# Where a weight matrix is split, and on which engine sums are formed, in a fused attention and two-layer kernel

## Chip, cores, metric

The kernel runs on one core of one Trainium2 chip. The metric is the device time of one execution in microseconds (us). Five engines work side by side: PE (TensorE, matrix products; the profile shows its weight loads as PEld), DVE (VectorE), ACT (ScalarE), POOL (GpSimd) and SP (SyncE, which here issues the DMAs).

## What is computed

Attention is followed by two feed-forward layers on the same 2304 tokens of width 512:

```python
x = attention(q, k, v, s)          # 4 x 8 heads, 576 rows, head width 64
h = x @ w_in                       # layer 1: 512 -> 2048
g = s * max(h, 0)**2 + b
x = g @ w_out                      # 2048 -> 512
a, b = x @ w_a, x @ w_b            # layer 2: 512 -> 1536, twice
out = (a * b) @ moe2_w_out         # 1536 -> 512
```

All is in float32. A product in full float32 is made of three products in the engine's reduced format: each operand is split into a high part (a cast on ACT) and a low part (operand minus high part, on DVE), and hi*hi, hi*lo and lo*hi are added up in PSUM. In layer 2 the products are moreover done by a scheme with seven block products in place of eight, as Strassen's, so sums and differences of blocks of the operands are needed as well, and these are split too.

## The kernel before

**Planner.** The kernel hands a list of operations, each with an engine, an estimated cost and a priority (a position in time, smaller first), to `Plan`. `Plan.order` (L120) plays them through once, with these costs, and takes at each moment the ready operation of the smallest priority; the instructions go out in that order. So the order on each engine is fixed before the kernel runs: an instruction whose operand is late holds up all that stands behind it on its engine. Buffers belong to a `Tag` (L31), which is a number of slots; a tag that is `in_order` gives its slots out in the order in which the buffers were declared, and an operation that needs a slot is not ready until one is free.

**Stages.** Up to 511 us attention and the first chunks of layer 1 share the engines. From 511 to 619 us layer 1 does its last two chunks (`last_two`, L898): 16 slices, in each 12 matmuls of `hh` and 12 of `yy`, of 512 columns. Between a slice's `hh` and its `yy` stand a relu on ACT (L830), a product on DVE (L841), an addition with cast on ACT (L844) and a subtraction on DVE (L846). This stage is called the tail of layer 1 below. From 619 to 886 us a and b are computed, in six rounds `i` of about 44 us: in each, `group(i, m, j)` (L1103) and `conv` (L1162) multiply the tokens by one slice of w_a (m = 0) and of w_b (m = 1). From 886 to 1016 us follows the product with moe2_w_out for two halves `j` of the tokens (`g_pair`, L1296), seven block products of 3 x 12 matmuls each, and from 1016 us on the rest of the tokens (`g_conv`).

**Slices of weights.** `w2_slice` (L1002) brings one slice of 1 MB in: a DMA into `t_wraw` (2 slots), a decoding from float64 in two or three passes (`decode`, L434: ACT L450, DVE or ACT L457/L453, DVE L459 and L462), four sums of blocks on POOL (L1017) into `sm` (`t_sum`, 1 slot), and then for `wa` (the blocks) and `ws` (the sums) a cast on ACT and a subtraction on DVE (L1021, L1022). Both land in `t_ring`, 4 slots. It is called for 12 slices of w_a and w_b, where round `i` prepares round `i + 1`, and by `wo_slice` (L1190) for the six slices of moe2_w_out; there 8 DMAs of 256 KB (L1197) then write `wa` and `ws` to `wo_dr` in DRAM, from where `wo_load` (L1229) takes them for the last product. In the kernel before, all six `wo_slice` have positions 432 to 462 and so lie in the tail of layer 1 with the two slices of round 0.

**Slots of `t_w`.** This tag has 16 slots of 8 KB per partition, in order. In layer 1 they hold its weights; in the rounds they hold 7 + 7 split blocks of tokens (`X`) and one more for `conv`, so 15; in the last product they hold `wo` (12) and the split blocks of a*b (`G`).

**Sums of a*b.** `g_sums` (L1269) takes four blocks R of a*b for each half `j` and each of three `ip`, and forms five sums on POOL (L1278 through `sub`, and L1290), each of 128 x 1024 elements: R00 = R01 - R00, d2 = R11 - R00, R01 = R11 - R01, R10 = R10 - R11, R10 = R10 + R00. Seven operands per `ip` go through `g_split` (L1262): a cast on ACT, a subtraction on DVE (L1265). The partial results of the seven products are added on DVE out of PSUM (L1331).

Of the kernel before, what the change touches and what calls it, by code (L numbers as in the profile page):

```python
# [14 lines left out]
ALU = mybir.AluOpType  # L15
# [12 lines left out]
PE, DVE, ACT, POOL, SP = "PE", "DVE", "ACT", "POOL", "SP"  # L28
# [205 lines left out]
def fused_kernel(  # L234
# [15 lines left out]
    nc = tc.nc  # L250
# [5 lines left out]
    NF1 = w1.shape[0]  # L256
# [7 lines left out]
    op = plan.op  # L264

    def as32(ap):
        return ap.bitcast(F32)
# [21 lines left out]
    def tag(pool, shape, dt, bufs, name, in_order=True):  # L289
        def make(n):  # L290
            p = pools[pool] if isinstance(pool, str) else pool
            return p.tile(shape, dt, tag=name, bufs=bufs, name=n)

        return Tag(make, bufs, in_order)
# [9 lines left out]
    t_w = tag(wpool, [P, 2, 2, DM], F32R, NF1, "w")  # L304
# [517 lines left out]
    for p in range(NPAIR):  # L822
        x_t[NCK - 1, p] = Buf(t_x, f"xlast{p}")
        op(SP, 0.4, 431.0, lambda p=p: nc.sync.dma_start(as32(x_t[NCK - 1, p].t), as32(xl_dr.t[p])),
           r=[xl_dr], w=[x_t[NCK - 1, p]], dma=262144)
# [147 lines left out]
    NFH = NF2 // 2  # L973
    t_ring = tag("ph2", [P, 4, 2, 2 * P], F32R, 4, "ring")
    t_wraw = tag("ph2", [P, 2, DM, 2], U32, 2, "wraw")
    t_sum = tag("ph2", [P, 4, 2 * P], F32, 1, "wsum")
    t_yraw = tag("ph2", [P, 2, 512], F32, 2, "yraw")
    t_su = Tag(lambda n: moe.tile([P, 2, 512], F32, tag="g", bufs=3, name=n), 3, False, t_g)
# [15 lines left out]
    def after(n0, deps):  # L994
        for o in plan.ops[n0:]:
            for d in deps:
                d.next.append(o)
                o.wait += 1

    ring = {}  # L1000

    def w2_slice(m, i, pos, n, src):  # L1002

        raw, sm = Buf(t_wraw, f"raw2_{m}{i}"), Buf(t_sum, f"sm{m}{i}")
        wa, ws = Buf(t_ring, f"wa{m}{i}"), Buf(t_ring, f"ws{m}{i}")
        ring[m, i] = wa, ws
        n0 = len(plan.ops)
        words = decode(raw, src, n % 2 == 1, pos, pos)

        def blk(q):  # L1010
            return words(1).bitcast(F32).rearrange("p a (b n) -> p (a b) n", n=2 * P)[:, q]

        for z, (q, x, y, f_) in enumerate((
            (0, lambda: blk(3), lambda: blk(2), ALU.add), (1, lambda: sm.t[:, 0], lambda: blk(0), ALU.subtract),
            (2, lambda: blk(0), lambda: blk(3), ALU.subtract), (3, lambda: blk(1), lambda: sm.t[:, 1], ALU.subtract),
        )):
            op(POOL, 0.75, pos + 0.1, lambda q=q, x=x, y=y, f_=f_: nc.gpsimd.tensor_tensor(out=sm.t[:, q], in0=x(), in1=y(), op=f_),  # L1017
               r=[(raw, "hi"), *([(sm, 0)] if q == 1 else [(sm, 1)] if q == 3 else [])], w=[(sm, q)])
        for t, k_, rd, src in ((wa, 0.0, (raw, "hi"), lambda: words(1).bitcast(F32).rearrange("p a (b n) -> p (a b) n", n=2 * P)),
                               (ws, 0.2, sm, lambda: sm.t)):  # L1020
            op(ACT, 1.08, pos + k_, lambda t=t, src=src: nc.scalar.copy(t.t[:, :, 0], src()), r=[rd], w=[(t, 0)])  # L1021
            op(DVE, 1.12, pos + k_, lambda t=t, src=src: nc.vector.tensor_tensor(  # L1022
                out=t.t[:, :, 1], in0=src(), in1=as32(t.t[:, :, 0]), op=ALU.subtract
            ), r=[rd, (t, 0)], w=[(t, 1)])
        after(n0, ready2)
# [162 lines left out]
    wo_dr = dram_buf([4, NFH // 2, P, 2, 2, 2, 2 * P], F32R, "wo_dr")  # L1188

    def wo_slice(i, pos):  # L1190
        w2_slice("o", i, pos, i, w2o[i])
        n0 = len(plan.ops)
        for g, names in enumerate(GROUPS):
            for z, n_ in enumerate(names):
                t, q = PLACE[n_]
                t = ring["o", i][t]
                op(SP, 0.35, pos + 0.5, lambda g=g, z=z, t=t, q=q: nc.sync.dma_start(  # L1197
                    as32(wo_dr.t[g, i // 2, :, z, i % 2]), as32(t.t[:, q])
                ), r=[t], w=[(wo_dr, (g, i, z))], dma=262144)
        after(n0, ready2)  # L1200

    PER = 60.0
    for i in range(NFH):
        wo_slice(i, 432.0 + 6.0 * i)
    for m in range(2):
        w2_slice(m, 0, 440.0 + 10.0 * m, m, w2ab[0, m])
    x_pair(0, 500.0)
    x_pair(1, BASE + 1.0)
    x_conv(BASE + 2.0)
    for i in range(NFH):  # L1210
        p0 = BASE + PER * i
        for m in range(2):
            group(i, m, 0, p0 + 8.0 * m)
        c0, g0 = (16.0, 24.0) if i + 1 < NFH else (32.0, 16.0)
        for m in range(2):
            conv(i, m, p0 + c0 + 4.0 * m)
        for m in range(2):
            group(i, m, 1, p0 + g0 + 8.0 * m)
        if i + 1 < NFH:
            for m in range(2):  # L1220
                w2_slice(m, i + 1, p0 + 4.0 + 20.0 * m, m, w2ab[i + 1, m])

    EP = BASE + PER * NFH
    ORDER = (("11", "11", 0), ("d2", "s2", 1), ("21", "12", 0), ("d3", "s3", 1), ("d1", "s1", 2), ("d4", "22", 1), ("22", "s4", 2))
# [37 lines left out]
    def g_split(j, n_, ip, pos, rd, src):  # L1262
        hl = G[j, n_, ip]
        op(ACT, 1.0, pos, lambda: nc.scalar.copy(hl.t[:, :, 0], src()), r=[rd], w=[(hl, 0)], late=0.1)
        op(DVE, 1.12, pos, lambda: nc.vector.tensor_tensor(  # L1265
            out=hl.t[:, :, 1], in0=src(), in1=as32(hl.t[:, :, 0]), op=ALU.subtract
        ), r=[rd, (hl, 0)], w=[(hl, 1)], late=0.08)

    def g_sums(j, pos):  # L1269
        for ip in range(NIP):  # L1270
            pr = pos + 0.2 * ip
            r = {(fh, T): R[j, fh, T, ip] for fh in range(2) for T in range(2)}
            key = {k_: (v_[0], v_[1][1]) for k_, v_ in r.items()}
            ap = {k_: v_[2] for k_, v_ in r.items()}
            d2 = Buf(t_sum if ip == 0 else t_yraw, f"d2{j}{ip}")

            def sub(k_, o, a, b, okey, rds):
                op(POOL, 2.3, pr + k_, lambda: nc.gpsimd.tensor_tensor(out=o(), in0=a(), in1=b(), op=ALU.subtract),  # L1278
                   r=rds, w=[okey])

            d2v = lambda d2=d2: d2.t.rearrange("p a n -> p (a n)").rearrange("p (a n) -> p a n", a=2)
            g_split(j, "11", ip, pr, key[0, 0], ap[0, 0])
            sub(0.0, ap[0, 0], ap[0, 1], ap[0, 0], key[0, 0], [key[0, 1]])
            sub(0.1, d2v, ap[1, 1], ap[0, 0], d2, [key[1, 1], key[0, 0]])
            g_split(j, "d2", ip, pr + 6.0, d2, d2v)
            g_split(j, "21", ip, pr + 12.0, key[1, 0], ap[1, 0])
            sub(10.0, ap[0, 1], ap[1, 1], ap[0, 1], key[0, 1], [key[1, 1]])
            g_split(j, "d3", ip, pr + 18.0, key[0, 1], ap[0, 1])
            sub(20.0, ap[1, 0], ap[1, 0], ap[1, 1], key[1, 0], [key[1, 1]])
            op(POOL, 2.3, pr + 20.1, lambda a=ap: nc.gpsimd.tensor_tensor(out=a[1, 0](), in0=a[1, 0](), in1=a[0, 0](), op=ALU.add),  # L1290
               r=[key[0, 0]], w=[key[1, 0]])
            g_split(j, "d1", ip, pr + 24.0, key[0, 0], ap[0, 0])
            g_split(j, "d4", ip, pr + 30.0, key[1, 0], ap[1, 0])
            g_split(j, "22", ip, pr + 36.0, key[1, 1], ap[1, 1])
# [233 lines left out]
```

## Time and profile before

| | us |
|---|---|
| median of 3 runs | 1036.35 |
| lowest and highest run | 1035.92, 1040.34 |
| the profiled execution, its own time | 1038.79 |
| span of its trace, first to last instruction | 1037.10 |
| PE busy | 982.1 |
| DVE busy | 776.2 |
| ACT busy | 552.1 |
| POOL busy | 219.2 |

The profile gives one execution, with each instruction's start, length, and what ended the idle time before it. PE's busy time is modelled from pipelined matmuls, so that one at full pace still shows small overlaps; the distance between the starts of blocks of matmuls is the better measure of pace. The granted clock of PE is 1.00 where it is at full speed.

### The profile page before, as it was taken

How to read it: one execution, taken by the hardware profiler on the slowest of the kernel's cores; microseconds unless marked ns; L12 is line 12 of the kernel's file. 1: busy time of each engine (PE TensorE's matmuls, PEld its weight loads, DVE VectorE, ACT ScalarE, POOL GpSimd, SP SyncE). 2: the span in 40 equal slices, each digit the busy share in tenths (PEclk: the TensorE clock that was granted, in tenths of full speed). 3: DMA queues.
4: the chain of work that ended last, by engine and by line, in shares of the span. 5: the costliest groups of instructions: out<-in, count | busy, mean ns of one | idle time of the engine just before them, and what ended most of it. 6: DMA issues, size and time to landing. Idle time of an engine off the chain costs nothing. (4 is left out here: it accounts for less than half of the span.)

```text
span 1037.1 us, 17316 instructions
## 1 busy us (share of the span) xinstructions
PE 982.1 (95%) x6664; PEld 877.6 (85%) x6664; DVE 776.2 (75%) x1153; ACT 552.1 (53%) x1025; POOL 219.2 (21%) x173
## 2 busy tenths in 40 slices
PE   4699999999999999999999879999999999999798
PEld 4598999999999999999877657888888888778678
DVE  6889764578788888887489977757576567877872
ACT  4779974568787878786356543313133121423331
POOL 4121001100000000000244524112011113955920
PEclk9999999999999999999999999999999999999899
DMA  9958523557769687866588633413222356955013
GB/s 231 225 159 226 143 82 67 120 134 172 153 137 188 135 159 157 159 142 116 188 307 295 206 101 109 170 68 122 88 86 95 128 172 244 365 188 177 0 61 102
DMA packets 159249, 160.12 MB, mean 154 GB/s; under 512 B 115008, under 2 KB 126016, under 8 KB 153280
## 3 DMA queue, kind: packets, MB, share of 16 engines
q1 hardware_dynamic: 159168, 159.03, 54.7%
q8 instruction: 52, 0.85, 0.3%
q14 instruction: 29, 0.24, 0.1%
HBM read 95.20 MB, written 37.52 MB: 128 GB/s over the span
## 5 line engine op out<-in xcount | busy, mean ns | idle before, releaser
L861 PE MATMUL h<-x_all,w 128*128 128x256 f32 x1344 | 180.3, 286 | 1.8 <-ACT r L830 1.0
L881 PE MATMUL y<-g,w 128*128 128x256 f32 x1344 | 181.1, 287 | 0.0
L861 PEld LDWEIGHTS h<-x_all,w 128*128 128x128 f32 x1344 | 168.8, 193 | 3.1 <-ACT r L830 1.2
L881 PEld LDWEIGHTS y<-g,w 128*128 128x128 f32 x1344 | 167.1, 191 | 1.5
L576 PE MATMUL av<-tr,vt 128*64 128x320 f16 (+4 forms) x1120 | 65.0, 274 | 12.7 <-DMA tr<-hl 7.5
L576 PEld LDWEIGHTS <-vt 128*64 128x64 bf16 x1120 | 54.5, 116 | 23.8 <-issue 8.5
L1095 PE MATMUL b<-x,wa 128*128 128x512 f32 x288 | 72.8, 390 | 0.0
L540 ACT ACTIVATE hl<-p,rc 128x256 f16<-128x256 f32 (+3 forms) x128 | 66.0, 559 | 4.4 <-DVE rc L557 4.4
L542 DVE SCALAR_TENSOR_TENSOR hl<-p,rc,hl 128x256 f16<-128x256 f32 (+3 forms) x128 | 65.8, 548 | 0.1
L1017 POOL TENSOR_TENSOR sm<-raw 128x256 f32<-128x256 f32 x24 | 26.4, 1100 | 183.9 <-DVE ws L1022 157.8
L1095 PEld LDWEIGHTS b<-x,wa 128*128 128x128 f32 x288 | 53.7, 188 | 10.8
L926 PE MATMUL yy<-gg,w 128*128 128x512 f32 x192 | 50.5, 408 | 11.2 <-DVE gg L846 8.6
L1130 ACT COPY su<-b 128x512 f32<-128x512 f32 x24 | 14.1, 587 | 85.2 <-PE b L1095 85.2
L1318 PE MATMUL pb<-g,wo 128*128 128x512 f32 x216 | 53.8, 403 | 5.4 <-DVE g L1265 2.8
L1120 DVE TENSOR_TENSOR su<-b,su 128x512 f32<-128x512 f32 x48 | 32.8, 687 | 31.6 <-PE b L1095 31.6
L926 PEld LDWEIGHTS yy<-gg,w 128*128 128x128 f32 x192 | 36.5, 194 | 23.2 <-DVE gg L846 11.9
L1318 PEld LDWEIGHTS pb<-g,wo 128*128 128x128 f32 x216 | 41.9, 195 | 14.9 <-ACT psu L1335 3.1
L1095 PE MATMUL b<-x0d,ws 128*128 128x512 f32 x216 | 54.2, 390 | 0.3 <-DVE su L1120 0.3
L1095 PE MATMUL b<-x1d,ws 128*128 128x512 f32 x216 | 53.7, 390 | 0.4 <-DVE su L1120 0.4
L626 PE MATMUL s<-kq 66*128 66x256 f32 (+1 forms) x128 | 43.5, 465 | 10.0 <-POOL vt L361 7.6
L914 PE MATMUL hh<-x_all,w 128*128 128x512 f32 x192 | 47.6, 400 | 3.1 <-ACT rr L830 3.1
L783 DVE TENSOR_REDUCE nm<-s 128x1 f32<-128x512 f32 (+1 forms) x64 | 36.9, 619 | 15.5 <-PE s L779 15.5
(379 smaller groups left out, 2087.6 us busy)
## 6 DMA issues: line engine op xcount, KB each, us to landing
raw<-in_w_dram SPq DMA_DIRECT2D x16, 1024.0 KB
raw<-in_w2ab_dram SPq DMA_DIRECT2D x12, 1024.0 KB
ab_dr<-at_all SPq DMA_DIRECT2D x24, 512.0 KB
wo<-wo_dr SPq DMA_DIRECT2D x12, 1024.0 KB
R<-ab_dr SPq DMA_DIRECT2D x24, 512.0 KB
rk<-in_k_dram SPq DMA_DIRECT2D x16, 576.0 KB
raw_o<-in_w2o_dram SPq DMA_DIRECT2D x6, 1024.0 KB
wo_dr<-wao SPq DMA_DIRECT2D x24, 256.0 KB
```

The lines of the kernel that those rows point to most:

```text
L540: nc.scalar.activation(o, i_, AF.Copy, scale=r_)
L542: nc.vector.scalar_tensor_tensor(out=o, in0=i_, scalar=r_, in1=place()[:, k0:k1, 0, :cols], op0=ALU.mult, op1=ALU.subtract)
L576: nc.tensor.matmul(ap.t[64 * h : 64 * h + 64, :w], vap(j, h, vi), t[:, j, a, h, :w], start=j == 0 and m == 0, stop=j == nkt - 1 and m == 4,)
L626: nc.tensor.matmul(o, qt[:66, x, h, ti * P : (ti + 1) * P], kt[:66, x, h, :w], start=True, stop=False)
L783: op(DVE, DVE_PS(w), pr, lambda c=c, w=w, nmx=nmx, bank=banks[c]: nc.vector.tensor_reduce(out=nmx.t[:, c : c + 1], in_=bank.t[:, :w], axis ...
L861: nc.tensor.matmul(o, w[:, wi, c, :], x_t[ck, c].t[:, xi], start=m == 0, stop=m == 3 * KC - 1)
L881: nc.tensor.matmul(o, w1_t[2 * fp + j].t[:, 1, wi, e * P : (e + 1) * P], g.t[:, gi, j], start=fp == 0 and e % 2 == 0 and j == wi == gi == ...
L914: nc.tensor.matmul(hp.t, w[:, wi, c, :], x_all[:, :, c, xi, :], start=m == 0, stop=m == 3 * KC - 1)
L926: nc.tensor.matmul(y_ps[e].t, w1_t[f].t[:, 1, wi, e * P : (e + 1) * P], g.t[:, gi].rearrange("p a n -> p (a n)"), start=f == m == 0, stop= ...
L1095: nc.tensor.matmul(o, wt.t[:, q, wi, kt * P : (kt + 1) * P], hl_of(kt, xi), start=first and n == 0, stop=last and n == 5, skip_group_check ...
L1120: op(DVE, 0.64, e, lambda: nc.vector.tensor_tensor(out=dst(), in0=bank.t, in1=a(), op=ALU.add), r=[bank, *reads], w=[key], late=0.08)
L1318: nc.tensor.matmul(banks[bi][dp].t, wv(i2, wi, dp), hl.t[:, i2, xi, :], start=n_ in fresh and ip == i2 == m == 0, stop=ip == NIP - 1 and i ...
```

## The change

- `wo_slice` is called from within the rounds: slice 0 in round 0, 1 in round 1, 2 and 3 in round 2, 4 in round 3, 5 in round 4, none in round 5, at positions 14 (and 36) after the start of the round, in place of 432 to 462.
- Its `wa` and `ws` come from a new tag `t_wv`, a view of `t_w` that shares its slots and its queue, in place of `t_ring`. As `t_w` has 15 of 16 slots taken in the rounds, `ws` of a slice can be written when the four DMAs of its `wa` have ended.
- `w2_slice` forms its sums on the engine that it is told: VectorE for the two slices of round 0, POOL for all others, with estimated costs of 0.42 and 0.95 in place of 0.75.
- `g_sums` forms its sums on VectorE, with an estimated cost of 1.12 in place of 2.3, and four of them in place of five: R10 = R10 - d2 in place of (R10 - R11) + R00. d2 is so read later, and its buffer held longer.

```diff
--- before
+++ after
@@ -973,6 +973,8 @@
     t_wraw = tag("ph2", [P, 2, DM, 2], U32, 2, "wraw")
+    t_wv = Tag(lambda n: t_w.make(n).rearrange("p a b n -> p (a b n)").rearrange("p (q z n) -> p q z n", q=4, z=2), NF1, True, t_w)
+    t_wv.queue = t_w.queue
@@ -999,10 +1001,10 @@
-    def w2_slice(m, i, pos, n, src):
+    def w2_slice(m, i, pos, n, src, home, sums_on):
 
         raw, sm = Buf(t_wraw, f"raw2_{m}{i}"), Buf(t_sum, f"sm{m}{i}")
-        wa, ws = Buf(t_ring, f"wa{m}{i}"), Buf(t_ring, f"ws{m}{i}")
+        wa, ws = Buf(home, f"wa{m}{i}"), Buf(home, f"ws{m}{i}")
@@ -1014,7 +1016,8 @@
-            op(POOL, 0.75, pos + 0.1, lambda q=q, x=x, y=y, f_=f_: nc.gpsimd.tensor_tensor(out=sm.t[:, q], in0=x(), in1=y(), op=f_),
+            f_eng, cost = (nc.gpsimd, 0.95) if sums_on == POOL else (nc.vector, 0.42)
+            op(sums_on, cost, pos + 0.1, lambda q=q, x=x, y=y, f_=f_, f_eng=f_eng: f_eng.tensor_tensor(out=sm.t[:, q], in0=x(), in1=y(), op=f_),
@@ -1188,7 +1191,7 @@
     def wo_slice(i, pos):
-        w2_slice("o", i, pos, i, w2o[i])
+        w2_slice("o", i, pos, i, w2o[i], t_wv, POOL)
@@ -1200,10 +1203,9 @@
     PER = 60.0
-    for i in range(NFH):
-        wo_slice(i, 432.0 + 6.0 * i)
+    WO_AT = ((0,), (1,), (2, 3), (4,), (5,), ())
     for m in range(2):
-        w2_slice(m, 0, 440.0 + 10.0 * m, m, w2ab[0, m])
+        w2_slice(m, 0, 440.0 + 10.0 * m, m, w2ab[0, m], t_ring, DVE)
@@ -1218,7 +1220,9 @@
             for m in range(2):
-                w2_slice(m, i + 1, p0 + 4.0 + 20.0 * m, m, w2ab[i + 1, m])
+                w2_slice(m, i + 1, p0 + 4.0 + 20.0 * m, m, w2ab[i + 1, m], t_ring, POOL)
+        for n, io in enumerate(WO_AT[i]):
+            wo_slice(io, p0 + 14.0 + 22.0 * n)
@@ -1275,7 +1279,7 @@
             def sub(k_, o, a, b, okey, rds):
-                op(POOL, 2.3, pr + k_, lambda: nc.gpsimd.tensor_tensor(out=o(), in0=a(), in1=b(), op=ALU.subtract),
+                op(DVE, 1.12, pr + k_, lambda: nc.vector.tensor_tensor(out=o(), in0=a(), in1=b(), op=ALU.subtract),
@@ -1286,9 +1290,7 @@
-            sub(20.0, ap[1, 0], ap[1, 0], ap[1, 1], key[1, 0], [key[1, 1]])
-            op(POOL, 2.3, pr + 20.1, lambda a=ap: nc.gpsimd.tensor_tensor(out=a[1, 0](), in0=a[1, 0](), in1=a[0, 0](), op=ALU.add),
-               r=[key[0, 0]], w=[key[1, 0]])
+            sub(20.0, ap[1, 0], ap[1, 0], d2v, key[1, 0], [d2])
```

## Rows read from the trace of the kernel before

**Rows 1.** Busy time of each engine in the three stages; columns in the first line

```profile
core 0: us, PE busy (x) PEld busy (x) DVE busy (x) ACT busy (x) POOL busy (x), PEclk, DMA share, GB/s
511.05:619.39 108.34, 93.96 (x387) 73.65 (x385) 98.72 (x96) 59.06 (x79) 50.41 (x36) 0.97 0.63 217
619.39:886.12 266.73, 264.57 (x1297) 223.63 (x1296) 183.01 (x230) 72.27 (x93) 54.56 (x49) 1.00 0.37 134
886.12:1015.99 129.87, 119.73 (x507) 97.13 (x506) 100.97 (x62) 45.34 (x48) 79.05 (x26) 0.96 0.42 154
```

**Rows 2.** PE's waits, 495 to 620 us: us in total, times, longest

```profile
PE yy L926 <- DVE gg L846: 8.6, 7, 2.1
PE hh L914 <- ACT rr L830: 3.1, 1, 3.1
PE yy L926 <- ACT gg L844: 2.6, 2, 2.1
```

**Rows 3.** Timeline of PE, near both ends of the tail: start, length, [idle before <- releaser]

```profile
519.81 7.34 PE L914 MATMUL hh<-x_all,w 128*128 128x512 f32 x24 [3.13 <-ACT rr L830]
...
615.18 4.37 PE L926 MATMUL yy<-gg,w 128*128 128x512 f32 x11 [0.28 <-DVE gg L846]
```

**Rows 4.** Chain of work that ended last, its longest piece: start, length, what

```profile
822.40 47.64 PE b L1095 x210
```

**Rows 5.** Timeline of POOL, then of ACT, ahead of PE's first wait in the tail

```profile
515.44 1.72 POOL L1017 TENSOR_TENSOR smo<-raw_o,smo 128x256 f32<-128x256 f32 x1
...
517.19 1.04 ACT L1021 CAST wso<-smo 128x1024 fp32r<-128x1024 f32 x1 [3.97 <-POOL smo L1017]
```

**Rows 6.** Instructions on raw_o alone, 495 to 620: DVE, ACT, POOL busy

```profile
495.00:620.00 125.00, 28.51 (x21) 17.00 (x15) 32.90 (x24) 0.97 0.63 218
```

**Rows 7.** The same for wso: DVE and ACT busy

```profile
495.00:620.00 125.00, 7.31 (x6) 6.33 (x6) 0.97 0.63 218
```

**Rows 8.** Busy time in a stretch of layer 1; columns as in Rows 1

```profile
300.00:480.00 180.00, 180.00 (x1700) 172.97 (x1698) 150.20 (x310) 142.93 (x298) 2.04 (x10) 1.00 0.75 151
```

**Rows 9.** Busy time in one round; columns as in Rows 1

```profile
734.60:778.50 43.90, 43.90 (x218) 37.30 (x217) 29.47 (x39) 11.83 (x14) 6.25 (x8) 1.00 0.28 102
```

**Rows 10.** Timeline of all engines where one round hands over to the next

```profile
704.11 0.33 SPq L446 DMA_DIRECT2D raw<-in_w2ab_dram  x1
...
705.84 0.86 POOL L1017 TENSOR_TENSOR sm<-raw 128x256 f32<-128x256 f32 x1 [26.76 <-DVE ws L1022]
...
709.08 1.18 ACT L450 ACTIVATE raw<-raw 128x1024 f32<-128x1024 f32 x1
...
715.40 1.21 DVE L1022 TENSOR_TENSOR wa<-raw,wa 128x1024 fp32r<-128x1024 f32 x1
...
717.84 1.55 PE L1095 MATMUL b<-x,wa 128*128 128x512 f32 x6
```

**Rows 11.** Timeline of SP's queue: the stores of one wa

```profile
517.58 2.38 SPq L1197 DMA_DIRECT2D wo_dr<-wao  x4
```

**Rows 12.** Waits of SP's queue, 615 to 700, on a store to DRAM

```profile
SPq L1049 <- DMA y_dr<-yyo: 1.4, 1, 1.4
```

**Rows 13.** PE's waits, 865 to 1037 us

```profile
PE pb L1318 <- DVE psu L1331: 4.0, 1, 4.0
PE pb L1318 <- DVE g L1265: 2.8, 1, 2.8
PE pb L1318 <- ACT psu L1335: 2.7, 1, 2.7
```

**Rows 14.** Sums of L1278, then subtractions of L1265, from 865 on: busy time (count)

```profile
865.00:1037.10 172.10, 72.55 (x24) 0.97 0.45 165
...
865.00:1037.10 172.10, 93.32 (x42) 0.97 0.45 165
```

**Rows 15.** Timeline of POOL, then of DVE, from 872 us

```profile
872.04 2.40 POOL L1278 TENSOR_TENSOR R<-R 128x1024 f32<-128x1024 f32 x1 [31.28 <-DVE g L1265]
...
872.48 3.04 DVE L1265 TENSOR_TENSOR g<-R,g 128x1024 fp32r<-128x1024 f32 x1
```

## The prediction, made before the changed kernel ran

> **What bounds the kernel now.** Read first where PE stands still, since PE is busy for 982.1 of 1037.1 us (the table above) and all of the layers' work ends on it. The busy times by stage [rows 1] show three different stages. In the rounds that compute a and b (619 to 886 us) PE is busy for 264.57 of 266.73 us: there is nothing to win there. In the tail of layer 1 (511 to 619) it has 93.96 of 108.34 us, and in the last product (886 to 1016) 119.73 of 129.87, with granted clocks of 0.97 and 0.96 against 1.00 in the rounds. How much is lost is better read from pace. A long unbroken piece of the chain of waits gives 47.64 us for 210 matmuls of 512 columns [rows 4], 0.2269 each, or 2.72 us for a block of 12. The tail holds 32 blocks (16 slices, `hh` and `yy`), 87.1 us at that pace: it loses 21.2. The last product holds 42 blocks (2 halves, 7 products, 3 `ip`), 114.3 us: it loses 15.6.
>
> Then the waits. In the tail PE waited 8.6 us in seven pieces for DVE's low part of `gg`, 3.1 for ACT's relu and 2.6 for ACT's `gg` [rows 2]: 14.3 us. The other 6.9 are pace: 24 matmuls took 7.34 us right behind the first wait, where 5.45 is full pace, and the last 11 took 4.37 in place of 2.50 [rows 3]. The mean granted clock of 0.97 [rows 1] says that a part of the stage was granted 1.2 in place of 2.4 GHz, and the slow pieces lie behind waits: a wait here cost more than itself. DVE is the bound here: 98.72 of 108.34 us busy [rows 1]. The first wait has another shape: ACT's relu stood behind a cast of `wso`, which waited 3.97 us for POOL's sums, the last of which took 1.72 us [rows 5] where the planner had 0.75. In the last product the waits are 4.0, 2.8 and 2.7 us, on DVE's adds, DVE's subtractions and an ACT copy [rows 13].
>
> **Part 1: w_out's six slices leave the tail.** With them go, from the tail, 21 DVE instructions on `raw_o` (28.51 us), 6 on `wso` (7.31), 21 ACT instructions (17.00 and 6.33) and 24 POOL sums (32.90) [rows 6, 7], besides 6 loads and 48 stores. Added are the sums of round 0's two slices on DVE, 8 at an unknown cost: bounded above by POOL's 0.86 for the same shape [rows 10], below by a quarter of DVE's 1.21 for four times the width [rows 10], 0.30. I take 0.42, nearer to the row of the same engine: 3.4 us. DVE then has 98.7 - 35.8 + 3.4 = 66 us, and less, since many of these were stretched by POOL (part 3). Over the 89 us that I give the stage that is 74%. In layer 1's earlier chunks DVE ran at 150.2 of 180 us, 83%, and PE did not stop at all, 180.00 of 180.00 [rows 8], with the same four steps between product and product. So the waits should go nearly all, and with them the clock's dips. I keep 2 us for filling and emptying the stage: 19 us gained, 21 at most. The lower bound is that only the first wait with its dip (3.1 + 1.9) and half of the rest (8.1) go: 13.
>
> **Part 2: they land in the rounds.** Clean durations for a slice are 1.21 to 1.24 us for each of four DVE passes and 0.7 for a fifth in every other slice, some 5.2 us, so 31 us on DVE over 267. A round has 29.47 of 43.90 us [rows 9]; with one slice it has 34.7 (79%), with two, as round 2 hands over, 39.9 (91%). ACT goes from 11.83 to about 15.7 and covers its part. The 48 stores and 6 loads go through SP's queue, 0.6 us for each issue [rows 11], 29 us in all, at a DMA share of 0.37 [rows 1]; `ab` stores stand behind them, and their slots are reused only 44 us later. New is that `ws` waits until the four stores of `wa` have landed: 2.38 us of issue [rows 11] and some 1.4 more, which is how long a load waited after the last issue of a store to DRAM [rows 12]; 3.8 us, where the planner's constants (L67 to L69) allow 4.5. Behind the waiting cast of `ws` on ACT stand the copies out of PSUM that PE needs.
>
> What can be late is the handover. The slice of w_b for the next round can be split only when the ring frees: its low `wa` ended at 716.61 (715.40 + 1.21) and PE took it up at 717.84 [rows 10], 1.2 us later. One or two passes of a w_out slice ahead of it, 1.2 to 2.4 us, push PE by 0 to 1.2 at each of five handovers: 0 to 6 us. I take 3. The bounds are -1, as the waits of 2.2 us in this stage may shrink with the sums that POOL leaves at its end, and 8 with the crowded handover of two slices.
>
> The Trainium skill warns (Perfetto Trace Analysis, "DMA Instruction — HWDGE (DVE, Sync)") that the semaphore of a DMA that writes to HBM can come late, which speaks against a wait on such stores. The 1.4 us above are of this kind; by them the rule costs nothing here, and if a store took 5 us longer it would still fit in the room worked out for the last rival.
>
> **Part 3: sums of a*b on DVE.** Before, POOL and DVE held each other up. A subtraction on DVE took 1.21 us where POOL was idle [rows 10], but 3.04 from 872.48 on, while a POOL sum ran from 872.04 to 874.44: the DVE one ended 1.08 after POOL's end [rows 15]. The 42 subtractions took 93.32 us, 2.22 each, and 24 of the 30 POOL sums 72.55, 3.02 each [rows 14]. After it, 42 splits at 1.22 are 51 us, 24 sums (four for each of 6 sets) at 1.2 are 29, 20 adds at 0.65 are 13: 93 us of the 138 between 870 and 1008, 67%. POOL has nothing. The sum on DVE is not in the trace at this shape without a cast; the nearest row, 1.21, has the same shape and two inputs, and POOL's 2.40 is the other end (24 x 1.2 = 29 us more, 88%, as busy as now). I take 1.2. The sums now stand in DVE's own queue ahead of the adds that free PSUM, each for 1.2 us at most, where 3 us stood before. d2's buffer, held longer, is needed next for a result one product (8 us) later. So I leave 2.6 of the 15.6 us: 13 gained, 15.6 at most, 6 at least.
>
> The Trainium skill has a rule for this too (SBUF — State Buffer, "Who interferes with whom"): a DVE instruction with two SBUF inputs and a GpSimd instruction that reads SBUF exclude each other for a whole instruction. The 1.08 above agree with it. It also speaks against part 2, where 24 sums on POOL come into the rounds; what that would make is the first rival.
>
> **Sum.** 19 - 3 + 13 = 29 us. Against the profiled execution, 1038.79 (span 1037.10 and 1.7 around it), that is 1009.8. The median of the runs is 2.4 below that execution; the gain is the same for both, so I take 1036.35 - 29 = 1007. By the bounds: 21 + 1 + 15.6 = 38 gives 998; 13 - 8 + 6 = 11 gives 1025.
>
> **Rivals.** (a) The rounds become DVE's. If a POOL sum blocks DVE for all its length, a round has 29.5 + 6.3 [rows 9] + 5.2 + 3.4 for each slice: 44.4 of 43.9 with one, 53 with two. The overrun is 4 x 0.5 + 9, and with 6 at the handovers 17 in place of 3: 1021. Against it: in the round shown, such a sum fell where DVE worked out of PSUM or waited, and PE lost nothing. 0.13. (b) The last product keeps its waits, because the sums stand in bursts in front of the adds at the change of halves: 5 gained of 15.6, 1015. For it: the longest wait now is on such an add [rows 13]. 0.10. (c) The change doesn't do what it says in the tail: PE waits there for the four steps themselves and not for DVE's load; then only the first wait with its dip and little more goes, 6, and 1020 results. Against it: the same steps and no wait in [rows 8]. 0.05. (d) Both (a) and (c), about 1034: 0.04. (e) Slower: the one free slot and the one slot of `sm`. A w_out slice holds `sm` through its sums (3.4), the stores (3.8), cast and subtraction (2.3), some 10 us, and the sums of the next w_a slice wait behind it. That slot stands unused for 26.76 us before each such pair [rows 10], so two slices (20) fit. It decides from a hold of over 27 us; as parts 1 and 3 bring 32, each of six slices must be over 6 us beyond that to end slower by 0.5%; at 8 each PE waits 48 us at the handovers, and 1052 results. 0.06.
>
> **Chances.** My forecast, 1007, stands for 1000 to 1013, with 0.62. The range 998 to 1022 takes in (a), (b) and (c) and leaves out (d) and (e). Faster by over 0.5% (what a measurement of this kernel can tell from no change) is all but (d) and (e): 0.90; within 0.5% is (d), 0.04; slower is (e), 0.06.
>
> **What would show it.** In the new profile the tail's `hh` and `yy` should take 88 to 91 us with DVE under 80% and no `raw_o` in it; the rounds 264 to 270 us, with DVE near 80%; L1265 should fall from 2.22 to about 1.22 us each; and the last product should take 115 to 119 us at a granted clock near 1.00. It is wrong if waits of PE on `wa` or `ws` appear at handovers, if L1265 stays over 2, or if `gg` still ends waits of PE in the tail.

## The result, and the profile after

The changed kernel takes 1006.35 us (median; 1004.75 to 1008.84), against 1037.51 for the kernel before on the same chip: a ratio of 0.9699, 95% interval 0.9667 to 0.9731, or 31 us faster (1037.51 is the median of four runs; three of them stand in the table of before). The profiled execution took 1007.19 us with a span of 1005.4, 31.7 less than the span before.

Busy time by stage, cut at the same places as [rows 1] (tail of layer 1, rounds, last product; the columns are the same):

```profile
511.02:599.61 88.59, 87.48 (x385) 72.08 (x386) 56.92 (x78) 39.14 (x59) 5.56 (x4) 1.00 0.15 50
599.61:870.14 270.53, 266.40 (x1298) 222.95 (x1296) 208.60 (x259) 93.22 (x113) 69.72 (x68) 1.00 0.55 192
870.14:984.40 114.26, 114.26 (x506) 94.60 (x505) 86.60 (x84) 46.58 (x49) 0.00 (x0) 1.00 0.53 200
```

The tail fell from 108.34 to 88.59 us (-19.75) and the last product from 129.87 to 114.26 (-15.61). The rounds rose from 266.73 to 270.53 (+3.80). What lies before and behind these stages kept its length. In the last product PE is busy for all of 114.26 us at a granted clock of 1.00: the pace of [rows 4] gives 114.3 for its 42 blocks, so nothing is left to win there. DVE's share of the tail fell from 91% to 64%; in the rounds it rose from 69% to 77%.

PE's waits of the changed kernel from 495 to 1010 us (total, times, longest), which answer to [rows 2, 13]:

```profile
PE b L1098 <- DVE u L1123: 2.3, 2, 1.5
PE b L1098 <- DVE su L1123: 1.7, 3, 0.9
PE hh L914 <- ACT rr L830: 1.1, 1, 1.1
```

No wait of PE in the tail ends on DVE any more, and none at all is left in the last product. What remains beside the 1.1 us in the tail is 4.0 us in the rounds, on adds out of PSUM; before, these were 1.5 us.

The subtractions of `g_split` and the sums on DVE, by form (count: shortest/median/longest in ns), which answer to [rows 14, 15]:

```profile
L1269 DVE TENSOR_TENSOR g0d<-d,g0d x3: 1218/1219/1220, 875.1 to 880.9; 128x1024 fp32r<-128x1024 f32 x3
L1269 DVE TENSOR_TENSOR g0d<-R,g0d x9: 1218/1221/1227, 887.7 to 912.3; 128x1024 fp32r<-128x1024 f32 x9
...
L1282 DVE TENSOR_TENSOR d<-R,R x6: 1225/1225/1226, 869.8 to 933.8; 128x1024 f32<-128x1024 f32 x6
```

Each takes 1.22 us, the longest as the shortest; before, the subtractions took 2.22 on the mean. A sum on DVE costs 1.22 too, half of POOL's 2.40 [rows 15].

### The profile page after: what moved, and what is told of

It is laid out like the page before. It is cut to its first block, busy times and chain, and to the rows that moved or that the text cites. A ratio compares the mean times of both kernels' runs of the same rounds, so it can differ in the third digit from the quotient of the medians.

```text
span 1005.4 us, 17274 instructions
## 1 busy us (share of the span) xinstructions
PE 972.1 (97%) x6664; PEld 872.9 (87%) x6664; DVE 745.7 (74%) x1185; ACT 553.4 (55%) x1025; POOL 111.0 (11%) x135
## 4 chain that ended last, share of the span: by engine, by line
PE 81%; DVE 8%; ACT 4%; DMA 4%; issue 3%; POOL 1%; SPq 0%; DVEq 0%; ACTq 0%; POOLq 0%
PE h L861 15%; PE y L881 15%; PE b L1098 13%; PE pb L1320 11%; PE av L576 6%; PE yy L926 4%; PE hh L914 4%; PE s L626 3%; PE s L778 3%; PE bc L1098 2%; PE pbc L1380 2%; DMA raw_o<-in_w2o_dram 1%; DMA raw<-in_w2ab_dram 1%; DVE su L1123 1%; ACT hl L540 1%
## 5 line engine op out<-in xcount | busy, mean ns | idle before, releaser
L1320 PE MATMUL pb<-g,wo 128*128 128x512 f32 x216 | 50.6, 389 | 0.0
L1098 PEld LDWEIGHTS b<-x0d,ws 128*128 128x128 f32 x216 | 40.2, 188 | 11.1 <-DVE su L1123 2.3
L1098 PEld LDWEIGHTS b<-x1d,ws 128*128 128x128 f32 x216 | 40.5, 188 | 9.2 <-DVE su L1123 0.9
L783 DVE TENSOR_REDUCE nm<-s 128x1 f32<-128x512 f32 (+1 forms) x64 | 36.9, 618 | 15.6 <-PE s L779 15.6
L830 ACT ACTIVATE r<-h 128x512 f32<-128x512 f32 x56 | 33.3, 595 | 25.0 <-PE h L861 24.7
L1133 ACT COPY su<-b 128x512 f32<-128x512 f32 x24 | 14.1, 586 | 58.5 <-PE b L1098 58.5
L926 PE MATMUL yy<-gg,w 128*128 128x512 f32 x192 | 45.6, 389 | 0.0
```

The costliest lines, as they stand in the source:

```text
L783: op(DVE, DVE_PS(w), pr, lambda c=c, w=w, nmx=nmx, bank=banks[c]: nc.vector.tensor_reduce(out=nmx.t[:, c : c + 1], in_=bank.t[:, :w], axis ...
L830: op(ACT, 0.49, e, lambda: nc.scalar.activation(r.t.rearrange("p a n -> p (a n)"), hp.t, AF.Relu), r=[hp], w=[r], late=0.1)
L926: nc.tensor.matmul(y_ps[e].t, w1_t[f].t[:, 1, wi, e * P : (e + 1) * P], g.t[:, gi].rearrange("p a n -> p (a n)"), start=f == m == 0, stop= ...
L1098: nc.tensor.matmul(o, wt.t[:, q, wi, kt * P : (kt + 1) * P], hl_of(kt, xi), start=first and n == 0, stop=last and n == 5, skip_group_check ...
L1320: nc.tensor.matmul(banks[bi][dp].t, wv(i2, wi, dp), hl.t[:, i2, xi, :], start=n_ in fresh and ip == i2 == m == 0, stop=ip == NIP - 1 and i ...
```

## The experiments

A stage's length is read here as in the table: from the first matmul of `hh`, of `b` and of `pb`, up to the first of `g_conv`. The runs were made on several chips, each beside runs of the kernel before on the same chip (medians of 1036.6 to 1039.2 us), so the ratios are to be compared and not the medians; gains in us below are against those runs. Times of each run:

| kernel | median, us | ratio to before (95%) | tail | rounds | last product |
|---|---|---|---|---|---|
| before (profile) | 1036.35 | 1 | 108.34 | 266.73 | 129.87 |
| changed | 1006.35 | 0.9699 (0.9667-0.9731) | 88.59 | 270.53 | 114.26 |
| e1_sums_only | 1019.59 | 0.9834 (0.9803-0.9864) | 106.35 | 265.83 | 114.26 |
| e2_move_only | 1030.21 | 0.9931 (0.9908-0.9953) | 87.74 | 270.83 | 138.31 |
| e3_five_on_dve | 1006.87 | 0.9713 (0.9680-0.9746) | 87.47 | 270.63 | 114.35 |
| e4_four_on_pool | 1028.16 | 0.9919 (0.9890-0.9948) | 87.47 | 271.02 | 137.52 |
| e12_move_early | 1024.93 | 0.9864 (0.9836-0.9892) | 87.45 | 273.62 | 129.95 |
| e5_tail_sums_dve | 1025.61 | 0.9863 (0.9839-0.9887) | 90.70 | 271.22 | 130.88 |
| e6_tail_cost | 1033.77 | 0.9951 (0.9931-0.9972) | 102.81 | 267.33 | 130.94 |
| e13_all_sums_dve_no_move | 1008.54 | 0.9728 (0.9713-0.9742) | 92.13 | 269.74 | 114.27 |
| e8_round_sums_dve | 1002.99 | 0.9676 (0.9662-0.9691) | 88.46 | 264.78 | 116.26 |
| e14_no_pool_sums_no_move | 1003.53 | 0.9670 (0.9641-0.9699) | 88.50 | 269.68 | 114.26 |

In e5, e13 and e14, twelve `yy` matmuls (2.7 us) come behind the first `b`, so there tail and rounds are compared as a sum: 375.1 before, 359.1 changed, 361.9 in e5, 361.9 in e13, 358.2 in e14, 353.2 in e8.

### Each half of the change alone

**e1_sums_only**: the kernel before with part 3 alone.

```diff
-                op(POOL, 2.3, pr + k_, lambda: nc.gpsimd.tensor_tensor(out=o(), in0=a(), in1=b(), op=ALU.subtract),
+                op(DVE, 1.12, pr + k_, lambda: nc.vector.tensor_tensor(out=o(), in0=a(), in1=b(), op=ALU.subtract),
...
-            sub(20.0, ap[1, 0], ap[1, 0], ap[1, 1], key[1, 0], [key[1, 1]])
-            op(POOL, 2.3, pr + 20.1, lambda a=ap: nc.gpsimd.tensor_tensor(out=a[1, 0](), in0=a[1, 0](), in1=a[0, 0](), op=ALU.add),
-               r=[key[0, 0]], w=[key[1, 0]])
+            sub(20.0, ap[1, 0], ap[1, 0], d2v, key[1, 0], [d2])
```

> The kernel before with part 3 alone (sums of a*b on VectorE, four in place of five; w_out's slices stay in the tail of layer 1). Theory: the two parts act in different stages and add up. The last product falls from 129.9 us to 114 to 116, its DVE subtractions from 2.22 us to 1.22 each; tail (108) and rounds (267) stay; the time falls by 14 to 16 us. Rival: the tail's lateness or the DMAs of the rounds carry into the last product, so that it stays over 120 and the time falls by less than 10.

**e2_move_only**: the changed kernel with this edit taken back, so that parts 1 and 2 stand alone.

> The changed kernel with the sums of a*b as before: five, on POOL. Theory: the tail takes 88 to 90 us, the rounds 269 to 272, the last product 128 to 132; the time falls by 15 to 17 us against before. Rival: the moved slices come late to the last product (their stores, their loads) and part 3 had hidden that: last product over 135, the time falls by less than 12.

e1 is 17.3 us faster than before (14 to 16 was expected), and its last product is 114.26 us: part 3 alone wins that stage wholly, 15.6 us. Tail and rounds are 2.0 and 0.9 us shorter too, where the theory had them stay. e2 is only 6.7 us faster. Its tail (87.74) and its rounds (270.83) are those of the changed kernel, but its last product takes 138.31 us, 8.4 more than before, where nothing of it was edited and 128 to 132 was expected. So the halves don't add up: 17.3 + 6.7 = 24, against 31 for both together.

PE's waits of e2_move_only from 860 us on:

```profile
PE pb L1322 <- DVE psu L1335: 5.1, 2, 4.2
PE pb L1322 <- DVE g0d L1269: 4.1, 1, 4.1
PE pb L1322 <- ACT psu L1339: 2.6, 1, 2.6
PE pb L1322 <- DVE g L1269: 2.5, 1, 2.5
PE pb L1322 <- DVE g1d L1269: 0.7, 1, 0.7
```

The wait of 4.1 us on `g0d`, at the second product, is new; the others were there before too, that on `psu` 1.1 us shorter ([rows 13], which leave out one of 0.7 on `g1d`). All waits together are 4.8 us more than before; the rest of the 8.4 is pace, at a mean granted clock of 0.93 where it was 0.96. No wait ends on a load of `wo`, so it is not that the moved slices come late. The origin of the new wait is in the order of the instructions, here in e2_move_only on PE, SP's queue, ACT, DVE, POOL and PE again (start, length, what, [idle before <- releaser]):

```profile
833.69 1.52 PE L1098 MATMUL b<-x1d,ws 128*128 128x512 f32 x6
...
840.49 2.88 PE L1098 MATMUL b<-x0d,ws 128*128 128x512 f32 x12
...
853.74 1.16 SPq L1159 DMA_DIRECT2D ab_dr<-at_all  x2
...
856.17 2.00 ACT L1268 CAST g<-R 128x1024 fp32r<-128x1024 f32 x2
...
861.69 1.22 DVE L1269 TENSOR_TENSOR g<-R,g 128x1024 fp32r<-128x1024 f32 x1
...
862.99 2.40 POOL L1282 TENSOR_TENSOR R<-R 128x1024 f32<-128x1024 f32 x1 [22.49 <-DVE g L1269]
...
869.38 5.63 PE L1322 MATMUL pb<-g,wo 128*128 128x512 f32 x24
...
879.37 5.06 PE L1322 MATMUL pb<-g0d,wo 128*128 128x512 f32 x11 [4.14 <-DVE g0d L1269]
```

POOL's first sum starts 6.4 us ahead of the first `pb`; before it was 14.1 us ahead (872.04 in [rows 15], the stage begins at 886.12). The stores of the first half's a*b come 15.6 us ahead of `pb`, where they came 22.8 ahead before. The first sum moreover waits for DVE's subtraction on the same block, which starts 5.5 us after ACT's cast (1.5 before), behind adds for PE's products. Four rows of before, on PE, SP's queue, ACT and DVE:

```profile
858.99 1.52 PE L1095 MATMUL b<-x1d,ws 128*128 128x512 f32 x6
...
863.35 1.68 SPq L1156 DMA_DIRECT2D ab_dr<-at_all  x2
...
869.23 2.00 ACT L1264 CAST g<-R 128x1024 fp32r<-128x1024 f32 x2
...
870.75 1.22 DVE L1265 TENSOR_TENSOR g<-R,g 128x1024 fp32r<-128x1024 f32 x1
```

In e2, round 5 begins to multiply by w_a for the second half of the tokens (`x1d`, 833.69) before it multiplies by w_b for the first (`x0d`, 840.49); before, `x1d` came up at 858.99, when the first half was nearly done. The likely reason: slice 5 of moe2_w_out, at position 864, stands ahead of w_b's slice of round 5, at 874, and the planner finds that one ready too late to keep the order. The next run tests this.

**e12_move_early**: e2 with slices 1 to 5 one place earlier, so that none stands before w_b of round 5.

```diff
-    WO_AT = ((0,), (1,), (2, 3), (4,), (5,), ())
+    WO_AT = ((0, 1), (2,), (3, 4), (5,), (), ())
```

> As the run that moves the slices alone (sums of a*b on POOL, five), but with w_out's slices one round earlier: 0 and 1 in round 0, 2 in round 1, 3 and 4 in round 2, 5 in round 3, none in rounds 4 and 5. The move alone gave a last product of 138.3 us where the kernel before has 129.9. Theory: in the move alone, slice 5 stands in front of round 5's slice of w_b, the planner then puts a group of the second token half ahead of w_b's of the first half, the first half of a*b is complete 15 us ahead of the last product in place of 23, and POOL's sums start too late. Here the planner's order of round 5 is that of the kernel before, so the last product takes 128 to 132 us and the time is 5 to 9 us under the move alone. Rival: POOL's sums are late for another reason (the load of w_out's blocks, DMA): the last product stays at 136 to 140 us.

Round 5 has the order of before (`x1d` comes up 27.2 us ahead of the first `pb`; before it was 27.1, in e2 35.7), POOL's first sum starts 14.1 us ahead of the first `pb`, and the last product has the length of before:

```profile
857.35 2.40 POOL L1282 TENSOR_TENSOR R<-R 128x1024 f32<-128x1024 f32 x1 [28.89 <-DVE g L1269]
```

```profile
871.47:1001.42 129.95, 119.08 (x507) 96.49 (x506) 100.81 (x62) 45.35 (x48) 78.98 (x26) 0.96 0.42 155
```

So the interaction of the two halves is the order of round 5. (e12 also stores most slices earlier; but no wait of PE in e2 ended on a load of `wo`, so earlier loads had nothing to win there.) With sums on POOL the order of e2 costs 8.4 us in the last product; with sums on DVE, which take half as long and stretch nothing, the same order, which the changed kernel has too, costs nothing (114.26). In exchange e12's rounds are 2.8 us longer than e2's (273.62 against 270.83); in time it is at 0.9864 of before, e2 at 0.9931.

### Which of part 3's two edits counts

**e3_five_on_dve**: the changed kernel with all five sums, on DVE.

```diff
-            sub(20.0, ap[1, 0], ap[1, 0], d2v, key[1, 0], [d2])
+            sub(20.0, ap[1, 0], ap[1, 0], ap[1, 1], key[1, 0], [key[1, 1]])
+            op(DVE, 1.12, pr + 20.1, lambda a=ap: nc.vector.tensor_tensor(out=a[1, 0](), in0=a[1, 0](), in1=a[0, 0](), op=ALU.add),
+               r=[key[0, 0]], w=[key[1, 0]])
```

> The changed kernel with the fifth sum back, on VectorE: six more subtractions of 1.22 us, 7.3 us of DVE. Theory: the engine counts and not the dropped sum; DVE has room in the last product (86.6 of 114.3 us), PE doesn't wait, the time stays within 2 us of the changed kernel. Rival: the dropped sum carries a share of the gain; the last product takes over 118 us and the time rises by 4 to 7 us.

**e4_four_on_pool**: the changed kernel with its four sums on POOL.

```diff
-                op(DVE, 1.12, pr + k_, lambda: nc.vector.tensor_tensor(out=o(), in0=a(), in1=b(), op=ALU.subtract),
+                op(POOL, 2.3, pr + k_, lambda: nc.gpsimd.tensor_tensor(out=o(), in0=a(), in1=b(), op=ALU.subtract),
```

> The changed kernel with its four sums on POOL in place of VectorE. Theory: POOL and DVE hold each other up; DVE's subtractions stay near 2 us each, POOL's sums near 3, the last product takes 121 to 128 us, and the time is 7 to 14 us over the changed kernel. Rival: it was the number of sums in POOL's chain, and a fifth less is enough: last product under 118 us, time within 3 us of the changed kernel.

With the fifth sum kept, the last product takes 114.35 us and the kernel 1006.87: its loss can't be told from nothing, for DVE has room. With four on POOL the stage takes 137.52, within 0.8 of e2's five. The engine decides and not the number. The expectation for e4 had this direction but not the size (121 to 128 for the stage, 7 to 14 us over the changed kernel; by the ratios it is 23 over): it left out the order of round 5, which e4 shares with e2.

### What POOL does to DVE in the last product

Moving the sums takes work from POOL, but it also shortens DVE's own subtractions. To separate the engine from the data, two kernels add to the changed one, in each `g_split` but two, work on POOL that nobody needs: 60 additions that read and write a scratch tile, or 120 memsets that only write it. A copy of one column of `g` ties each to its place.

```diff
+        if n_ in ("11", "21", "d3", "d1", "22"):
+            def load():
+                nc.gpsimd.tensor_copy(scr[:, 416:417], as32(hl.t[:, 0, 1, 0:1]))
+                for _ in range(2):
+                    nc.gpsimd.tensor_tensor(out=scr[:, :416], in0=scr[:, :416], in1=scr[:, :416], op=ALU.add)
+            op(POOL, 3.0, pos, load, r=[hl])
```

**e10_pool_reads** is this one:

> The changed kernel with POOL given work of no use in the last product: behind 30 of the 42 splits a copy of one column and two additions of 128 x 416 on a tile of its own, which read SBUF twice and write it. Theory: a POOL instruction that reads SBUF and a DVE one with two SBUF inputs exclude each other; the mean of DVE's subtractions there rises from 1.22 us to 1.5 to 2.2, and the time rises by 0 to 10 us. Rival: POOL slowed DVE only through common data and order; the mean stays under 1.3.

**e11_pool_writes** has `for _ in range(4)` and `nc.gpsimd.memset(scr[:, :416], 0.0)` in its place:

> As the run with useless POOL work in the last product, but behind the same 30 splits POOL copies one column and then fills 128 x 416 four times, which writes SBUF and reads nothing. Compared with that run alone and in the last product alone (125.6 us there, DVE's subtractions 1.37 to 1.67 us): the tile they need changes the order of the first 500 us in both. Theory: it is POOL's reading that shuts DVE out; DVE's subtractions go back to 1.2 to 1.3 us and the last product to 114 to 117. Rival: any access of POOL to SBUF slows DVE, or POOL holds PE up by the block of weights that it keeps; subtractions over 1.35 or a last product over 120.

Both begin with a memset of the tile, which comes with a start of the tail 8 to 12 us later and rounds 4 to 5 us longer (1033.14 and 1022.80 us in all), so that e10's time says nothing on its expected rise of 0 to 10 us; only the last product is compared. For e10, the added instructions by form, DVE's busy time on its subtractions, the stage, and PE's longest wait:

```profile
L1279 POOL TENSOR_TENSOR scr<-scr x60: 875/882/1920, 880.2 to 1006.9; 128x416 f32<-128x416 f32 x60
```

```profile
886.48:1012.04 125.56, 58.26 (x40) 0.97 0.51 187
```

```profile
886.48:1012.04 125.56, 119.03 (x507) 95.81 (x505) 103.93 (x85) 45.78 (x49) 93.80 (x85) 0.97 0.51 187
```

```profile
PE pb L1329 <- DVE g1d L1272: 5.0, 1, 5.0
```

And for e11 the first three:

```profile
L1279 POOL MEMSET scr<- x120: 439/446/452, 876.3 to 990.2; 128x416 f32 x120
```

```profile
882.59:996.86 114.27, 48.17 (x40) 1.00 0.54 198
```

```profile
882.59:996.86 114.27, 114.27 (x507) 94.60 (x506) 86.51 (x84) 46.38 (x49) 73.40 (x140) 1.00 0.54 198
```

With POOL busy for 73.40 us on writes alone, DVE's subtractions take 1.20 us each (48.17 / 40), PE never waits, and the stage is 114.27, as without this load. With POOL reading, they take 1.46 (58.26 / 40), the additions on POOL go from 0.88 up to 1.92, PE waits 5.0 us, and the stage takes 125.56. That is a little under the 1.5 to 2.2 expected, and far over the rival's 1.3. The two loads are of one size when unhindered: 60 additions at 0.88 are 53 us, 120 memsets at 0.446 too; that POOL was busier in e10 (93.80) is in the main the stretching itself, as its additions took 70.0 in all. The writes, with POOL at 64% of the stage, left no trace at all. This is what the Trainium skill states (SBUF — State Buffer, "Who interferes with whom"): a DVE instruction with two SBUF inputs contends with a GpSimd one that reads SBUF, not with one that only writes it. The traces agree, at 1.46 against 1.20 us.

### What the tail waited for

**e5_tail_sums_dve**: the kernel before, nothing moved, but the sums of the tail's eight slices on DVE.

```diff
-            op(POOL, 0.75, pos + 0.1, lambda q=q, x=x, y=y, f_=f_: nc.gpsimd.tensor_tensor(out=sm.t[:, q], in0=x(), in1=y(), op=f_),
+            f_eng, eng_, cost = (nc.vector, DVE, 0.42) if m == "o" or i == 0 else (nc.gpsimd, POOL, 0.75)
+            op(eng_, cost, pos + 0.1, lambda q=q, x=x, y=y, f_=f_, f_eng=f_eng: f_eng.tensor_tensor(out=sm.t[:, q], in0=x(), in1=y(), op=f_),
```

> The kernel before with the sums of the eight slices that lie in the tail of layer 1 on VectorE (cost 0.42), nothing moved. Theory: the tail is bound by DVE's own work; 24 more sums come to the clean 89 us or so that it has there, the tail stays at 102 to 112 us, and the time within 5 us of before. Rival: it was POOL, by the waits for its sums and by what it takes from DVE; then the tail falls to 90 to 98 us and the time by 10 to 18.

The tail with all of moe2_w_out's slices in it, and PE's waits from 495 to 625 us (the second lies in the rounds):

```profile
509.65:600.35 90.70, 86.81 (x375) 70.81 (x374) 85.73 (x119) 56.58 (x75) 4.51 (x4) 0.98 0.72 249
```

```profile
PE yy L926 <- DVE gg L846: 3.4, 1, 3.4
PE b L1096 <- DVE u L1121: 1.4, 1, 1.4
PE yy L926 <- ACT gg L844: 0.4, 1, 0.4
```

The theory of the prediction, that PE waits because DVE is loaded to 91%, falls here: DVE is now busy for 85.73 of 90.70 us, 95%, with 30 sums more, and the seven waits on `gg` have become one. Without its 30 sums (11.85 us) DVE has 73.9 us of work, where it had 98.72 before. Seven instructions lie outside the stage here, worth at most 8.6 us (1.23 each). So at least 16 us of DVE's load in the tail (98.72 - 73.9 - 8.6) was no work of its own: its instructions were longer while POOL formed the sums. On the 16 subtractions that make `gg` it is seen directly; before, then e5:

```profile
511.05:619.39 108.34, 16.09 (x16) 0.97 0.63 217
```

```profile
509.65:600.35 90.70, 12.33 (x16) 0.98 0.72 249
```

**e6_tail_cost**: the kernel before with only the planner's cost of these sums put right, so that only the order can change.

```diff
-            op(POOL, 0.75, pos + 0.1, ...
+            op(POOL, 1.5 if m == "o" or i == 0 else 0.75, pos + 0.1, ...
```

> The kernel before, the planner's cost of POOL's sums in the tail set to 1.5 us (the trace shows 1.1 to 1.8) in place of 0.75; nothing else. Theory: the planner's short cost made only the first wait of PE (3.1 us and its dip, 5 in all), as ACT stood behind a late sum; the tail falls by 3 to 6 us. Rival: no share is due to the cost, the tail stays within 2 us of 108.

The first wait, 3.1 us for ACT's relu behind a cast that stood for POOL [rows 2, 5], is gone, and the waits on `gg` remain:

```profile
PE yy L926 <- DVE gg L846: 10.5, 8, 2.6
PE yy L926 <- ACT gg L844: 0.6, 1, 0.6
```

By the runs this is worth 5.1 us (0.49%, interval 0.28 to 0.69%), about two fifths of what e5 gives in the two stages together (375.1 - 361.9 = 13.2). The rest goes with the sums themselves. Whether it is the stretching alone or also the sums' own length on POOL, 0.75 to 1.7 us against 0.42, no run here tells apart.

### What the move is worth, and what the rounds lost

**e13_all_sums_dve_no_move**: e5 with part 3 (the edit of e1).

> The kernel before with the sums of the tail's eight slices on VectorE and part 3, w_out's slices left in the tail: the whole change without the move. Theory, after the run with the tail's sums on VectorE gave a tail of 90.7 us: the move adds next to nothing once POOL is out of the tail; tail and rounds together take 359 to 363 us (changed kernel 359.1), the last product 114 to 116, and the time is within 5 us of the changed kernel. Rival: with POOL off the last product as well the load that stayed in the tail shows; the time is 6 us or more over the changed kernel.

It takes 1008.54 us, a ratio of 0.9728 against 0.9699 for the changed kernel: the ratios are 0.29% apart, 3 us, and their intervals overlap. So moving the slices adds some 3 us to moving the sums (2.8 by tail and rounds together), which the times alone don't tell from nothing.

**e8_round_sums_dve**: the changed kernel with the sums of all later slices on DVE as well.

```diff
-        w2_slice("o", i, pos, i, w2o[i], t_wv, POOL)
+        w2_slice("o", i, pos, i, w2o[i], t_wv, DVE)
...
-                w2_slice(m, i + 1, p0 + 4.0 + 20.0 * m, m, w2ab[i + 1, m], t_ring, POOL)
+                w2_slice(m, i + 1, p0 + 4.0 + 20.0 * m, m, w2ab[i + 1, m], t_ring, DVE)
```

> The changed kernel with the sums of the rounds on VectorE too, at 0.42 us planned, so that POOL forms no sums of weights at all. Theory: the 4 us that the rounds lost came from POOL's sums, planned at 0.95 us and up to 1.9 long where DVE works; rounds of 265 to 268 us in place of 270.5, the time 2 to 5 us under the changed kernel. Rival: DVE's own load in the rounds is the cost; rounds of 270 to 276 us.

The rounds, and one form of the sums:

```profile
601.05:865.83 264.78, 263.98 (x1298) 223.50 (x1296) 220.38 (x317) 93.83 (x114) 11.65 (x8) 1.00 0.56 198
```

```profile
L1020 DVE TENSOR_TENSOR smo<-raw_o x12: 411/417/425, 661.2 to 835.5; 128x256 f32<-128x256 f32 x12
```

DVE has more to do than in the changed kernel (220.38 us against 208.60, 83% against 77%), and the rounds are 5.8 us shorter, 2 below those of before. So the 3.8 us that the change loses in the rounds are no matter of DVE's load: they go with POOL's sums (e8 changes their planned cost with their engine, from 0.95 to 0.42; no run separates the two). In the time 2.0 us of this are given back in the last product (116.26, with a wait of PE of 1.3 us on an add). One handover of the changed kernel shows how (all engines; sums that take 0.74 to 0.86 us alone take 1.61 and 1.88 beside DVE):

```profile
775.30 1.61 POOL L1020 TENSOR_TENSOR sm<-sm,raw 128x256 f32<-128x256 f32 x1
...
776.87 1.88 POOL L1020 TENSOR_TENSOR sm<-raw 128x256 f32<-128x256 f32 x1
...
779.49 1.05 ACT L1024 CAST ws<-sm 128x1024 fp32r<-128x1024 f32 x1 [5.47 <-POOL sm L1020]
...
780.57 1.23 DVE L1025 TENSOR_TENSOR ws<-sm,ws 128x1024 fp32r<-128x1024 f32 x1 [1.33 <-ACT ws L1024]
...
782.45 1.67 PE L1098 MATMUL b<-x,ws 128*128 128x512 f32 x6 [1.50 <-DVE u L1123]
```

ACT stands 5.47 us for the sums, with its copies out of PSUM behind it; DVE stands 1.33 us for ACT, with its adds behind it; and PE stands 1.50 us for such an add.

**e14_no_pool_sums_no_move**: the same without the move (e13 with every slice's sums on DVE).

> The kernel before with every sum of weights and of a*b on VectorE (part 3 included), w_out's slices left in the tail of layer 1: the run with the rounds' sums on VectorE, less the move. Theory: the move is worth what DVE's full tail costs at its end and no more, 3 to 6 us; tail 91 to 93 us, rounds 265 to 269, last product 114 to 117, time 1004 to 1009. Rival: the move is worth nothing, tail and rounds together under 356 us (353.2 with the move) and the time under 1004; or it is worth over 7 us, time over 1010.

It takes 1003.53 us, ratio 0.9670, and e8 0.9676: no difference. The theory expected 1004 to 1009 and the rival under 1004, so the time lies just on the rival's side; but tail and rounds together take 358.2, where the rival had under 356, and that is the theory's figure (91 to 93 and 265 to 269). In these two stages the move is worth 5.0 us (353.2 in e8); e8 gives 2.0 back in the last product, and its tail begins 2.6 us later, behind stages that no edit touches (their length differs by up to 4.7 us between the profiles of the table). So with no sums on POOL the move is worth nothing that the times can tell, and at most 5 us. Both runs are below the changed kernel, by 2 to 3 us, and the intervals of all three ratios overlap.

## Why the prediction was right, point by point

The forecast was 1007 us and the kernel takes 1006.35. So close it is partly by luck: the gain was 31.2 us, 2 more than forecast, and a fourth run of the kernel before put its median 1.2 us over the 1036.35 that the forecast started from. The three terms, 19 - 3 + 13 = 29, came out as 19.75 - 3.80 + 15.61 = 31.6. The sizes held; two of the three reasons did not.

**Part 1, size right, reason wrong in part.** The gain was read from pace (21.2 us lost, 2 kept back), which doesn't depend on the reason. The step that failed is "DVE is the bound here". A busy share was taken for work, though at least 16 of its 98.72 us were instructions made longer by POOL's sums (e5). The prediction named this ("many of these were stretched by POOL") and gave it no size: it left DVE with 66 us in the new tail, and DVE has 56.92. In e5 DVE is at 95% in the tail, and PE loses 6.4 us there (90.7 less 31 blocks of 2.72 us), against 21.2 before. The comparison with layer 1's earlier chunks, 83% and no wait [rows 8], pointed the same way, since POOL has only 2.04 us there; the prediction put the difference down to DVE's 83% against 91%. What it described for part 3, DVE and POOL holding each other up [rows 15], was at work in the tail too. The first wait was read rightly: e6 gives 5.1 us for the cost alone, where the prediction's lower bound had 3.1 + 1.9 for it.

**Part 2, size right, place wrong.** The loss is 3.8 us where 3 was taken, but not as one or two DVE passes ahead of a slice of w_b: no wait of PE's matmuls ends on `wa` or `ws` in the changed kernel (one weight load waits 0.4 us for `ws`), and e8 makes DVE busier and the rounds shorter. That 3 comes near 3.8 is luck. It is nearer to rival (a), POOL's sums and DVE holding each other up, at a fifth of the price that it was given (17). The cost of the sums of round 0 on DVE, 0.42, was 0.417 in e8.

The landing of the stores was taken at 1.4 us after their issue. In the changed kernel, SP, then ACT:

```profile
794.93 1.78 SPq L1200 DMA_DIRECT2D wo_dr<-wao  x4
...
801.33 1.05 ACT L1024 CAST wso<-smo 128x1024 fp32r<-128x1024 f32 x1 [6.72 <-DMA wo_dr<-wao]
```

From the end of the issues (796.71) it took 4.6 us. The hold is 6.4 us from the first issue, where 3.8 was taken. ACT stood for such stores four times, 12.6 us in all, and saw them landed 3.6 to 6.5 us after the end of their issues; PE lost nothing by it that its waits show. The [rows 12] that gave 1.4 are of stores of 128 KB, at a DMA share of 0.40 while SP waited. Here four stores of 256 KB, 1 MB, were on their way, and the DMA engines were full (the last two numbers are their share and GB/s):

```profile
796.71:801.33 4.62, 4.62 (x28) 4.06 (x27) 4.62 (x6) 0.00 (x1) 0.34 (x1) 1.00 1.07 315
```

That is 1.46 MB in the 4.6 us, so the moving of data is enough to explain the time. Whether the semaphore of a store to HBM also came late, of which the Trainium skill warns (Perfetto Trace Analysis, "DMA Instruction — HWDGE (DVE, Sync)"), no run here shows.

**Part 3, mechanism right, undersized.** The subtractions fell to 1.22 as said, the sums cost 1.22 where 1.2 was taken, and the clock came back to 1.00. The 2.6 us kept back for sums in front of adds were not needed: PE doesn't wait in this stage. The term was also taken as independent of the move, and it isn't. In the order that the move brings, part 3 is worth 24 us (e2 to the changed kernel), alone 15.6 (e1): without it, the move would have given 8.4 us back in the last product. A reading of the working is off too, with nothing resting on it: DVE at 88% was called "as busy as now", where it was busy for 113.30 of these 138 us before, 82%.

**The rivals.** (b) and (c) did not come, and so not (d): no wait is left in the last product, and the tail keeps one of 1.1 us. (e) did not come: no wait of PE's matmuls ends on a slice of weights. Of the marks named ahead two were missed, both narrowly: the rounds took 270.53 us (264 to 270 was named) and the last product 114.26 (115 to 119).

## What to carry to other kernels

An engine's busy time in a profile can hold time that another engine costs it, here at least 16 of 98.72 us; before a stage is called bound by its load, compare the same instruction's length with and without the neighbour. Where VectorE and GpSimd both read SBUF with tensor-tensor work, giving GpSimd's part to VectorE can take more off VectorE than it puts on: here half of the 31 us came from moving 24 sums, and of the tail's gain most came without moving any slice (e5: 13.2 us in tail and rounds together, where the whole change has 16.0). In a kernel with a planned order, run the halves of a change singly: an edit in one stage reordered another, and only the other half made that free.

## What the runs showed of the hardware that was not expected

- A 128x256 float32 sum takes 0.417 us on DVE, the longest 0.43; on POOL 0.74 to 0.86 us alone and up to 1.88 beside DVE. For 128x1024 it is 1.22 against 2.40.
- POOL at 64% of a stage with memsets alone left DVE's two-input instructions at 1.20 us; additions on POOL made them 1.46.
- Four stores of 256 KB to DRAM were seen by their waiter 3.6 to 6.5 us after the end of the issues; in the case of 4.6 us the DMA engines moved 315 GB/s meanwhile.
- DVE at 95% busy in a stage fed PE with waits of 3.8 us in 90.7 (e5).
